# Six of eight GpSimd drains taken out behind the experts' scatters

## The chip, the cores and the metric

One core of one Trainium2 chip runs the whole program: TensorE (matrix products), VectorE, ScalarE, GpSimd and SyncE, and 16 DMA engines that they share. The metric is the device time of one execution in microseconds (us), as the median of several runs. In the profile the engines are called PE (TensorE), PEld (TensorE's weight loads), DVE (VectorE), ACT (ScalarE), POOL (GpSimd) and SP (SyncE); POOLq is GpSimd's sequencer, which takes the instructions in their written order and hands them to the engine.

## What is computed

A gated linear recurrence over 768 steps for 4 x 8 heads, whose output, 3,072 tokens of 384 numbers, goes through a layer of 8 experts. Each token goes to one expert alone.

```python
for t in range(S):                       # attention: a complex state per head
    S_re, S_im = ar * S_re - ai * S_im + k[t] v[t]^T, ar * S_im + ai * S_re
    y[t] = q[t] @ S_re
x = y.transpose(0, 2, 1, 3).reshape(3072, 384)
logits = x @ w_gate                      # 8 experts
expert_idx = argmax(logits); gate_w = softmax(logits)[expert_idx]
for e in range(8):
    xe = x[expert_idx == e]
    ye = relu(xe @ w1[e]) @ w2[e]        # 384 -> 1024 -> 384
    out[expert_idx == e] = gate_w * ye
```

## The kernel before

The program has two stages. The first (to about 220 us) is the recurrence in chunks of 128 steps; at its end every token has been sent by GpSimd's indirect DMAs into `xs_hbm`, one block of rows for each expert. The second stage, which the change touches, is the experts' layer. It runs over the experts as *ranks*, r = 0 to 7, the fullest expert first.

For a rank, SyncE loads the rows and the weights (`loads`), VectorE turns the rows (`turned`), and TensorE makes the first layer. `fast1` forms it from sums and differences of blocks, seven products in the place of eight; the sums of weights (tile `ws`) are GpSimd's, those of rows (also in `ws`) are VectorE's, and those of results (`um`) VectorE's too. The second layer is `fast2`, called for rank r - 1 while r is at its first layer. It multiplies 3 x 2 blocks with a scheme of fifteen products, written out step by step in `FIFTEEN` (line 114). A step "W7 12-0" is a difference of weight blocks 12 and 0 into W7 (block 13), made by GpSimd (line 998); "H..." is the same for hidden values, by VectorE; "P5 11+13" is a product of hidden block 11 with weight block 13 into bank 5, four matmuls on TensorE, each two instructions in the trace; "C..." are copies by ScalarE and "A..." sums by VectorE; "G..." scales a result into a `yo` tile. Blocks 0 to 5 are the rank's own weights (`w2b`) or hidden values (`ht`); the others are scratch, which lies in `w2b` or `wA` tiles and in `htA`. W7 and W5 are each written twice in a rank, so the second writing has to follow the product that reads the first: for W7 that is "P2 12+13", for W5 "P1 6=11". The second W5 and W7 are read by "P5 3+11" and "P5 11+13".

When 128 tokens of a rank are done, `sent` (line 782) has GpSimd send the rows of `yo` to their places in the output by an indirect DMA (line 673; the *scatter*). The tokens of ranks 0 to 4 beyond 384 are worked in two shared tiles (`shared`, called at r = 1 and r = 4); their scatters take the row numbers from `hs`, the others from `hg`. Some `yo` tiles lie in memory named `mask` and `turn`.

Behind each rank's work the loop adds a drain of GpSimd (line 1059): `nc.gpsimd.drain()`. It names the marks "scattered" and "drained" to the planner, so that it stays behind the scatters that were added before it and drains stay in order among themselves; the instruction itself carries no semaphore wait and no engine waits for it. It is an instruction of GpSimd's sequencer, and what is written behind it for GpSimd waits until it is over.

All operations of the stage are collected in a `Plan` (`M.add`), each with what it reads and writes, and then issued in the order that `EXPERTS` (line 86) lists by hand: 994 numbers to the base 36, the places of the operations in the collection. Each engine takes its own in that order. Where a helper makes the sums and products, the trace has the helper's line: 200 for every two-operand sum, 770 for `product`.

Of the kernel before, what the change touches and what calls it, by code (L numbers as in the profile page):

```python
# [18 lines left out]
N, DM, E, F = B * S, H * D, 8, 1024  # L19
# [64 lines left out]


EXPERTS = """
0 1 2 3 4 g 7 c 9 1e 38 h i l o p r u v 8 1q n m x t 1r z q 10 a w s 13 11 16 14 17 j 18 19 b 12 1n 5 1i 1u y 1a 15 1y 22 1o
1v 1f 1z 20 1s 1x 1p 6 26 21 24 23 25 1h 28 1b 1w 2a f 1g 27 2b 2c 2e 2i 2d 2g 2f 1j 2m k 2h 2n 2k 1c 2s 29 2v 2u 2j 2l 2t 2x
e 1t 2q 2y 31 2r ev 2z 4y 3h 3o 3i 3p 56 33 34 3s 3t 3k 3r 3l 4z 50 3m 2p 2o 2w 57 5a 30 32 54 3n 3j 35 58 59 3u 3v 3w 3y 3x
3z 41 3q 40 44 45 48 46 3a 72 47 4a 5b 39 3b 74 49 4b 42 4e 5e 43 4f 4d 4c 4k 4l 3c 3e 7c 5c 5d 7d 5g 4g 55 5f 5i 3d 5h 1k 5l  # L90
51 52 53 7e 4n 4h 5n 4j 5m 5o 75 5j 7f 4t 7h 5p 4x 5q 73 1d 36 5k 5u d 7b 5r 4m 6h 5s 1m 5w 5x 6a 5t 5y 60 5z 4s 61 6i 37 62
63 6q 64 65 66 7k 7i 5v 4q 6s 6r 76 6b 6c ay 6d 6j 4u 67 6t 4w 7j 6y b2 4v 6e 6f 6k 6l 6m 6n 6g 7m 4i 7q az 4p 7l 6u 6v 6w 7n
8s 7r 90 6x 6z 92 7o 7p 7s b7 8t 8u 7t 7u 7g 7y 7v 4o ik 91 94 93 7z b0 80 77 81 82 84 96 6o 95 97 4r 83 68 87 9a 98 99 7w 86
85 88 8b 8a 7x 8g 8j 89 8h 8k ab 8e 8f 9f 9c 9g 8y 8z 8v b9 8w 8x 9h 8m 8p 9b 9i ba 8n 8i 9d 9e ac b6 bf 9k 9o 8c 9j 9q 9l 9m
9r 9s 9u ak bd be a4 9t 9w 9n 9v 9y 7a 9x 9p 3g a5 9z a6 a7 al ad 8q 69 6p 8r bb a0 a1 bc b8 am cn co a8 cq cp cr an 79 a9 aa
ae ct b1 as af ag ao ap aq 8o ah aw bh bl bi bj bk bn f5 f3 b3 ax bg 8d a2 bm ar cu bp cv bq at cx bo br cw cs bt bu cy bx 8l
by bv f8 d1 cz d0 d3 d2 d4 bw c1 bz c0 c3 70 ai d5 d9 bs c4 f4 c2 cc d7 c9 cb ce c5 d6 d8 f6 ca ci c7 da db dc e6 cm dd cg e7
df de c6 dg dh dj c8 ex b5 dl dm 71 a3 dn do f7 dp di dq aj ch dk 78 dr au dt dv ds ew ef eg du dw fa dz e0 e2 ez ey cj e1 dx
f0 e3 e8 f2 e4 e9 ck eh ei ej en e5 ek el cd ea eb gj fb 1l em ec eq b4 eu fe ff cf fd fg gg gh it in fh av dy ed ee cl go eo
gq ep f9 il gp gs gr gu fi fj gt 3f fk gw fl gv fm fc gm gn fn fq fr fs er ft gi gk is gl gx h0 fu fy fv fw g2 fx fo no fp gy  # L100
gz h1 g0 g8 g1 fz g9 iv gb g6 gc h2 im g7 hz gd h3 h4 gf h5 h6 h8 hc h7 he iz g3 i0 np nq nr h9 ha hd hf es hg ga hh hi f1 hb
hj hk hl ip io ir hm g4 et ho hs j0 hn ht j1 hv ia i1 i8 hp ge hu i9 ib ns hw ig hx i2 hy k9 i3 i4 i5 j4 ix ic g5 hq j5 j8 iw
iy j6 id ie if mb iu ih ke j7 ja j9 jb j2 jc jd jg kf k6 k7 jh j3 kg je ji jj kc kd jk jl jm ki kh kk kj kl jo i6 jp jn jt km
jq js jf jr ko kn kp kq jw jz jv jx k8 k3 kt ku mc jy ks k1 kr ka kb lp kv li kw ky kx nt l2 kz md l4 lq l0 l3 ma mj l5 ly mh
m0 l6 l7 l8 l1 l9 la nu mi mk lb lz lc ld lj lk me ll k2 lr k5 m1 nv mf m6 k4 ml le lf hr i7 ju lm ln ls lt lu lv mg mm mn mo
lo m2 m3 mp m4 mq mu ms mr mv m5 k0 mt nw nx m7 ny nz o0 mw o1 my n2 mz n0 ps n3 mx o4 n1 lg n4 n7 pt o2 n5 pu o3 o5 pv ii iq
n6 n8 o6 na ij nc o8 ng p7 ni n9 o7 nh pw ne lh nk oa nf nl ob nj oc od p0 nn oe o9 og ok lw p8 nm of nb om oh oo nd oi on lx
m8 m9 q0 q1 pg oq op os oj or ou q2 q3 q4 q5 ot p1 ol ow ov ox ph p3 p4 p5 p9 p2 pi pj po pa pb pc px q8 pd qa pk p6 pl q9 pm
py pz pn pp qb qc pe qd qh q6 rc oy oz qj qx qe ql qf qk qn q7 qm qp qg qo qi r4 qr qq qy qs r0 r5 rd qt qu qz qv r1 r2 r3 re
rj pf pq r6 r7 rf r8 r9 ra pr qw rb rg rh ri rk rl  # L110
"""


# [73 lines left out]
def gateloop_then_moe(ctx, tc, gates, qk, gates_u, qk_u, v_u, v, wg, w1, w2, out):  # L187
    nc = tc.nc
# [13 lines left out]
    def const(shape, nm, val=None, dt=FP32):  # L202
        t = consts.tile(shape, dt, name=nm)
        if val is not None:
            nc.gpsimd.memset(t, val)
        return t
# [52 lines left out]
    lg = const([128, NT, E], "lg")  # L259


    with ExitStack() as att:
        ap = att.enter_context(tc.tile_pool(name="ap", bufs=1))

        def buf(nm, n, shape, dt=FP32):
            return [ap.tile(shape, dt, name=f"{nm}{i}") for i in range(n)]
        bAB, bZ = buf("AB", NB, [128, 2 * G * TU]), buf("Z", NZ, [128, G * 2 * TU])
        bC, cz = buf("C", NB, [128, G * TU]), buf("cz", NC, [128, G * 2 * TU])
        cm = buf("cm", 2, [112, 2 * 2 * TU])
        nc.vector.memset(cm[0][32:64], 0.0)  # L270
        vb = buf("v", NV, [128, 3, DM + D * len(SWAPPED)])
        am = buf("am", 4, [128, 4, 128])
        kt = buf("kt", 2, [128, 2, 384])
# [422 lines left out]
        with tc.manual_schedule():  # L696
            for u in range(NU):
                front(u)
                b, t0, t1 = UNITS[u]
# [7 lines left out]
                if u == NU - 3:  # L707
                    fa = early()
# [10 lines left out]
            for i in P.order(ORDER):  # L719
                o = P.ops[i]  # L720
# [11 lines left out]
    with ExitStack() as ms:  # L732
        mp = ms.enter_context(tc.tile_pool(name="mp", bufs=1, reuse_waits="tile"))
# [10 lines left out]
        ht = buf("ht", 2, [128, FT, 384])  # L744
        hl = buf("hl", 2, [128, FT, 128])
# [3 lines left out]
        hg = buf("hg", 3, [128, 3, 2])  # L749
        hs = buf("hs", 2, [128, 2])  # L750
# [15 lines left out]
        def pe(dur, fn, r, w):  # L766
            on_pe.append(M.add("PE", dur, fn, r, w, after=tuple(on_pe[-1:])))
# [182 lines left out]
        def tile2(r, j, k, k0=0):  # L950
            s = r % 2
            w, kw = w2_of(r)
            for h2 in range(2):
                def f(h2=h2):
                    for f_ in range(4 * h2, 4 * h2 + 4):
                        nc.tensor.matmul(bank[k][:, 0:DM], lhsT=ht[s][:, f_, j * 128 - k0:j * 128 - k0 + 128], rhs=w[:, f_ * DM:f_ * DM + DM],
                                         start=(f_ == 0), stop=(f_ == FT - 1))
                pe(2.6, f, (kw,) + tuple(("ht", s, f_, x) for f_ in range(4 * h2, 4 * h2 + 4) for x in range(2 if j else 1)), (("K", k),))
            finish(k, hg[r % 3][:, j, :], (("hg", r % 3),))
# [76 lines left out]
        def first_layer(r):  # L1036
            turned(r)
            if r == 0:
                late()
            (fast1 if r in FAST1 else layer1)(r)  # L1040

        with tc.manual_schedule():
            M.add("SP", 0.0, lambda: None, (), ("perm",))
            loads(0)
            for r in range(E + 1):
                if r + 1 < E:
                    loads(r + 1)
                if r < E:
                    first_layer(r)
                if r == 0:  # L1050
                    tile2(0, 2, 4, 256)
                if r == 1:
                    shared(0, 7)
                if r > 1:
                    fast2(r - 1)
                if r == 4:
                    shared(1, 5)
                if r < E:
                    M.add("POOL", 1.0, lambda: nc.gpsimd.drain(), ("scattered",), ("drained",))
                if r == 3:  # L1060
                    pe(0.2, lambda: nc.tensor.matmul(bank[5][0:1, 500:501], lhsT=okm, rhs=one, start=True, stop=True), ("okm",), (("K", 5),))
                    M.add("DVE", 0.2, lambda: nc.vector.tensor_scalar(out=again, in0=bank[5][0:1, 500:501], scalar1=127.5, scalar2=None, op0=ALU.is_lt), (("K", 5),), ("again",))
                if r == 4:
                    pe(0.5, lambda: flag.append(nc.values_load(again[0:1, 0:1], min_val=0, max_val=1, skip_runtime_bounds_check_because="0 or 1")), ("again",), ())
            for i in M.order(EXPERTS):
                M.ops[i]["fn"]()


    with tc.If(flag[0] > 0, preferred_fallthrough_block=False), ExitStack() as fs:  # L1069
        fp = fs.enter_context(tc.tile_pool(name="fp", bufs=1))  # L1070
# [5 lines left out]
        with tc.For_i(0, S, TB) as i0:  # L1076
            a = fp.tile([128, 2, B, G, TB], FP32, name="fa")
# [9 lines left out]
            af = a.rearrange("p u b g t -> p u (b g t)")  # L1087
# [12 lines left out]
            for t in range(TB):  # L1100
# [6 lines left out]
                z = {}  # L1107
# [5 lines left out]
                kv = fp.tile(shape, FP32, name="kv")  # L1113
# [14 lines left out]
        with tc.For_i(0, NT, 1) as ti:  # L1128
# [11 lines left out]
            l = fp.tile([128, E], FP32, name="l")  # L1140
            nc.vector.tensor_copy(l, bank[1][:, 0:E])
            m = fp.tile([128, 1], FP32, name="m")
            nc.vector.tensor_reduce(m, l, axis=AX, op=ALU.max)
            nc.vector.tensor_scalar(out=l, in0=l, scalar1=m, scalar2=None, op0=ALU.subtract)
            ex = fp.tile([128, E], FP32, name="fex")
# [5 lines left out]
            m2 = fp.tile([128, 1], FP32, name="fm2")  # L1151
# [4 lines left out]
            for e in range(E):  # L1156
# [4 lines left out]
                hh = fp.tile([128, FT, 128], FP32, name="hh")  # L1161
                for f_ in range(FT):
                    hb = bank[2 + f_ // 4][:, (f_ % 4) * 128:(f_ % 4) * 128 + 128]
                    for d in range(DT):
                        c = d * F + f_ * 128
# [57 lines left out]
```

## Time and profile before

| what | us |
|---|---|
| runs | 464.96, 465.85, 469.82 |
| median | 465.85 |
| profiled execution | 467.38 |
| its span, first to last instruction | 465.7 |
| mean granted TensorE clock | 0.994 of full speed |

The page's part 1 gives the busy time of each engine. TensorE is the busiest; GpSimd is busy for less than half of the span. Times in the rows are us from the span's start, durations of groups in ns where that is said. A row of a timeline is one instruction or several of a kind in succession: start, duration, engine, line, operation, written tile <- read tiles, shape, count, and in brackets the idle time of the engine ahead of it with what the profile takes for the releaser. A drain is work of the sequencer, not of the engine, so it is no busy time and stands in no timeline of the engine; it is found by its line.

### The profile page before, as it was taken

To read this page: it belongs to the slowest core of one execution; us is meant where nothing else is said; L and a number is where in the kernel's file an instruction comes from. 1 tells how busy PE (TensorE), PEld (TensorE's weight loads), DVE (VectorE), ACT (ScalarE), POOL (GpSimd) and SP (SyncE) were. 2 spreads that over 40 slices of the span, in tenths; PEclk is the share of its full clock that TensorE was granted. 3 is DMA by queue.
4 is the path that set the end of the run, shared out by engine and by line. 5 is a ranking of instruction groups with operands and counts; after the bars stand their busy time and mean duration, and the time that the engine had idled before them with its cause. 6 is when DMAs were issued, how large, how long until landed. Compare 5 with 4: busy or idle time off the path is not lost. (4 is left out here: it accounts for less than half of the span.)

```text
span 465.7 us, 12727 instructions
## 1 busy us (share of the span) xinstructions
PE 408.0 (88%) x5186; PEld 370.1 (79%) x5186; DVE 342.4 (74%) x623; ACT 290.7 (62%) x541; POOL 213.3 (46%) x256
## 2 busy tenths in 40 slices
PE   0142999989979998999999999899999999999994
PEld 0022788778869787898689799899997999999994
DVE  6999999999998999752443765475765655786762
ACT  5999999999998988743011333464636336346432
POOL 8100021027201545422044923666975949569664
PEclk9999999999999999999999999899999999999999
DMA  8355692866486662772793097804467152000102
GB/s 273 136 188 151 170 363 75 262 167 212 89 297 145 214 166 104 203 238 106 213 323 105 2 265 220 320 1 170 150 185 247 37 190 100 1 1 36 67 18 82
DMA packets 31554, 73.27 MB, mean 157 GB/s; under 512 B 19955, under 2 KB 21900, under 8 KB 28160
## 3 DMA queue, kind: packets, MB, share of 16 engines
q1 hardware_dynamic: 28160, 62.49, 44.2%
q0 software_dynamic: 3184, 9.86, 5.6%
q8 instruction: 43, 0.70, 0.6%
q14 instruction: 23, 0.19, 0.1%
q10 hardware_dynamic: 144, 0.03, 0.0%
HBM read 55.65 MB, written 12.29 MB: 146 GB/s over the span
## 5 line engine op out<-in xcount | busy, mean ns | idle before, releaser
L200 POOL TENSOR_TENSOR Z<-Z,C 128x1152 f32<-128x1152 f32 (+2 forms) x7 | 16.0, 2289 | 118.3 <-DVE Z L200 64.1
L200 DVE TENSOR_TENSOR um<-bank,um 128x432 f32<-128x432 f32 (+6 forms) x84 | 46.3, 566 | 31.5 <-PE bank L770 30.4
L770 PE MATMUL bank<-xrt,w1b 128*128 128x216 f32 (+6 forms) x336 | 68.6, 334 | 0.0
L770 PEld LDWEIGHTS bank<-xrt,w1b 128*128 128x128 f32 x336 | 58.2, 191 | 1.5 <-issue 0.6
L556 POOL DMA_INDIRECT xs_hbm<-xg,slot x24 | 32.4, 1352 | 37.3 <-issue 14.4
L300 ACT ACTIVATE AB<-AB 128x1152 f32<-128x1152 f32 (+5 forms) x46 | 45.5, 998 | 3.9 <-DVE first L613 1.8
L1009 ACT COPY bank<-ht 128x512 f32<-128x512 f32 x48 | 28.0, 589 | 22.5 <-DVE htA L200 14.4
L200 POOL TENSOR_TENSOR wA<-wA,w2b 128x512 f32<-128x512 f32 x22 | 28.2, 1289 | 25.6 <-PE bank L770 23.4
L422 PE MATMUL bank<-order,cz 128*128 128x128 f32 x60 | 11.1, 296 | 28.7 <-DVE cz L200 22.0
L200 DVE TENSOR_TENSOR am<-bank,mask 128x512 f32<-128x512 f32 x48 | 31.5, 679 | 3.6 <-PE bank L443 3.6
L200 DVE TENSOR_TENSOR Z<-Z,AB 128x1152 f32<-128x1152 f32 (+4 forms) x20 | 31.7, 1589 | 0.8 <-ACT AB L300 0.3
L770 PE MATMUL bank<-w2b,ht 128*128 128x128 f32 x240 | 31.2, 280 | 0.0
L435 PE MATMUL bank<-Z 48*64 48x128 f32 (+1 forms) x576 | 29.8, 254 | 1.2 <-DVE Z L200 1.2
L422 PEld LDWEIGHTS bank<-order,cz 128*128 128x128 f32 x60 | 7.0, 147 | 29.9 <-issue 22.3
L770 PE MATMUL bank<-ws 128*128 128x216 f32 (+6 forms) x168 | 30.7, 332 | 0.1
L723 ACT ACT_TABLE_LOAD x23 | 29.5, 1283 | 1.7 <-PEq L1208 1.3
L473 PE MATMUL bank<-am,v 128*48 128x128 f32 x384 | 26.1, 280 | 5.0 <-DVE am L200 5.0
L770 PEld LDWEIGHTS bank<-w2b,ht 128*128 128x128 f32 x240 | 29.7, 197 | 0.0
L435 PE MATMUL bank<-cz 48*64 48x64 f32 (+1 forms) x576 | 29.3, 261 | 0.4 <-DVE am L200 0.4
L770 PEld LDWEIGHTS bank<-ws 128*128 128x128 f32 x168 | 28.5, 190 | 0.4 <-POOL ws L200 0.4
L921 ACT ACTIVATE ht<-um 128x368 f32<-128x368 f32 (+9 forms) x42 | 20.9, 512 | 9.0 <-DVE um L200 9.0
L473 PEld LDWEIGHTS bank<-am,v 128*48 128x48 f32 x384 | 21.5, 126 | 5.8 <-DVE am L200 5.2
(250 smaller groups left out, 1158.9 us busy)
## 6 DMA issues: line engine op xcount, KB each, us to landing
w1b<-in_w_dram SPq DMA_DIRECT2D x7, 1536.0 KB, 7.5
w2b<-in_w_dram SPq DMA_DIRECT2D x7, 1536.0 KB, 10.3
AB<-in_gates_u_dram SPq DMA_DIRECT2D x6, 1152.0 KB, 5.9
Z<-in_qk_u_dram SPq DMA_DIRECT2D x6, 1152.0 KB, 7.8
v<-in_v_u_dram SPq DMA_DIRECT2D x8, 792.0 KB, 6.3
wA<-in_w_dram SPq DMA_DIRECT2D x4, 768.0 KB, 5.7
xs_hbm<-htA SPq DMA_DIRECT2D x2, 1045.0 KB, 9.1
xr<-xs_hbm SPq DMA_DIRECT2D x12, 156.0 KB, 4.8
```

The costliest lines, as they stand in the source:

```text
L200: return (eng or nc.vector).tensor_tensor(out=o, in0=a, in1=b, op=op)
L300: lambda: nc.scalar.activation(o, i, func=f, scale=scale, bias=bias, **kw), r, w, tag)
L422: nc.tensor.transpose(KT[part][:, g * 128:g * 128 + 128], wide[part][:, g, 1], order)
L435: nc.tensor.matmul(SC[h % 2][y:y + 64, g * 128 + x:g * 128 + 128], lhsT=wide[part][side(h), g, 1, x:x + 64], rhs=wide[part][side(h), g, 0, ...
L473: nc.tensor.matmul(YT[side(h), (h // 2) * 128:(h // 2) * 128 + 128], lhsT=values(h), rhs=am[2 * par + h % 2][:, h // 2, :], start=(c == 0 ...
L556: i = nc.gpsimd.indirect_dma_start(out=xs_hbm[:, :], out_offset=bass.IndirectOffsetOnAxis(ap=R[slot][:, c:c + 1], axis=0), in_=xg[:, (g0 + ...
L723: nc.scalar.preload_act_table_set("natural_log_exp_and_others" if P.cur == "LE" else "trig_and_small")
L770: nc.tensor.matmul(o, lhsT=l, rhs=x, start=start, stop=True, skip_group_check=True)
L921: M.add("ACT", 0.00094 * 2 * (hi - lo) + 0.16, lambda o=o, i=i: nc.scalar.activation(o, i, func=ACT.Relu), keys, ko)
L1009: M.add("ACT", 0.5, lambda o=blocks(bank[n], 1)[0], i=HO[int(a)]: nc.scalar.copy(o, i), HK[int(a)], (("K", n),))
```

## The change

The drain is added for r = 6 and r = 7 alone, the last two ranks. The six others leave the collection of operations, so the numbers of all later ones fall by one to six, and the list `EXPERTS` is written anew: it is the old list without the numbers 49, 115, 253, 391, 533 and 667 (in base 10), and the rest renumbered; the order of the remaining 988 operations is the same. No operation is added or moved.

```diff
 EXPERTS = """
-0 1 2 3 4 g 7 c 9 1e 38 h i l o p r u v 8 1q n m x t 1r z q 10 a w s 13 11 16 14 17 j 18 19 b 12 1n 5 1i 1u y 1a 15 1y 22 1o
+0 1 2 3 4 g 7 c 9 1d 36 h i l o p r u v 8 1p n m x t 1q z q 10 a w s 13 11 16 14 17 j 18 19 b 12 1m 5 1h 1t y 1a 15 1x 21 1n
...
 """
...
                 if r == 4:
                     shared(1, 5)
-                if r < E:
+                if r in (6, 7):
                     M.add("POOL", 1.0, lambda: nc.gpsimd.drain(), ("scattered",), ("drained",))
```

## Rows read from the trace of the kernel before

**Rows 1.** The page's part 1: busy time, share of the span, instructions.
```profile
PE 408.0 (88%) x5186; PEld 370.1 (79%) x5186; DVE 342.4 (74%) x623; ACT 290.7 (62%) x541; POOL 213.3 (46%) x256
```

**Rows 2.** Waits of PEld, 228 us to the end: us, times, longest us.
```profile
PEld bank L1030 <- issue: 5.6, 28, 0.3
PEld bank L770 <- POOL wA L200: 2.7, 2, 2.1
PEld bank L770 <- DVE htA L200: 0.6, 1, 0.6
PEld bank L770 <- POOL ws L200: 0.4, 1, 0.4
```

**Rows 3.** Table by stages: us; PE, PEld, DVE, ACT, POOL busy; PEclk, DMA, GB/s.
```profile
282.00:296.00 14.00, 12.06 (x108) 11.87 (x106) 7.92 (x19) 6.61 (x21) 4.94 (x5) 1.00 0.77 276
```

**Rows 4.** TensorE's timeline from 286 us: start, us, line, tiles, count [idle before].
```profile
286.66 1.06 PE L770 MATMUL bank<-wA 128*128 128x128 f32 x8
...
292.02 1.95 PE L770 MATMUL bank<-w2b,htA 128*128 128x128 f32 x16
295.92 1.67 PE L770 MATMUL bank<-wA 128*128 128x128 f32 x8 [1.94 <-POOL wA L200]
...
299.09 1.91 PE L770 MATMUL bank<-xrt,w1b 128*128 128x204 f32 x8
```

**Rows 5.** GpSimd's timeline from 286 us.
```profile
286.67 0.96 POOL L673 DMA_INDIRECT out_dram<-yo,hs  x1 [3.24 <-DVE mask L200]
287.63 1.30 POOL L200 TENSOR_TENSOR w2b<-w2b,w2b 128x512 f32<-128x512 f32 x1
294.60 1.26 POOL L200 TENSOR_TENSOR wA<-wA,w2b 128x512 f32<-128x512 f32 x1 [5.66 <-PE bank L770]
```

**Rows 6.** Line 1059, drains starting near 286 and 374 us (durations in ns).
```profile
L1059 POOLq DRAIN  x1: 8020/8020/8020, 286.5 to 286.5; - x1
...
L1059 POOLq DRAIN  x1: 9685/9685/9685, 374.7 to 374.7; - x1
```

**Rows 7.** DMA issues: the two scatters of shared tiles, us to landing.
```profile
out_dram<-yo,hs POOLq DMA_INDIRECT x1, 7.7
...
out_dram<-mask,hs POOLq DMA_INDIRECT x1, 7.5
```

**Rows 8.** Table by stages around 298 us; the granted clock is the third from last.
```profile
296.00:298.00 2.00, 2.00 (x11) 2.00 (x12) 0.09 (x1) 0.00 (x0) 1.92 (x2) 0.60 1.01 430
298.00:300.00 2.00, 2.00 (x11) 1.99 (x10) 0.00 (x0) 0.00 (x0) 1.92 (x3) 0.55 0.95 337
300.00:302.00 2.00, 2.00 (x13) 2.00 (x12) 0.73 (x3) 1.33 (x5) 2.00 (x2) 1.00 0.18 32
```

**Rows 9.** GpSimd's timeline: ranks 2 and 4, behind their drains.
```profile
341.82 0.99 POOL L673 DMA_INDIRECT out_dram<-yo,hg  x1 [1.27 <-issue]
...
376.68 0.92 POOL L673 DMA_INDIRECT out_dram<-mask,hs  x1 [0.16 <-DVE wA L200]
384.51 2.50 POOL L200 TENSOR_TENSOR wA<-wA,w2b 128x512 f32<-128x512 f32 x2 [6.92 <-PE bank L770]
```

**Rows 10.** TensorE's timeline from 377 us.
```profile
377.29 1.06 PE L770 MATMUL bank<-wA,htA 128*128 128x128 f32 x8
...
385.83 1.16 PE L770 MATMUL bank<-wA,ht 128*128 128x128 f32 x8 [0.34 <-POOL wA L200]
```

**Rows 11.** VectorE's timeline from 289 us.
```profile
289.15 0.64 DVE L200 TENSOR_TENSOR ws<-xrt 128x204 f32<-128x204 f32 x2
...
292.03 0.36 DVE L200 TENSOR_TENSOR ws<-xrt,ws 128x204 f32<-128x204 f32 x1
...
294.95 1.14 DVE L200 TENSOR_TENSOR ws<-xrt,ws 128x204 f32<-128x204 f32 x1
301.24 0.29 DVE L200 TENSOR_TENSOR mask<-bank,part 128x128 f32<-128x128 f32 x1 [5.15 <-ACT part L1012]
```

**Rows 12.** VectorE's groups by line and form: busy us, mean ns of one.
```profile
L200 DVE TENSOR_TENSOR htA<-htA,wA 128x512 f32<-128x512 f32 x1 | 3.1, 3105 | 0.0
```

More of the change, by code (lines that the diff above doesn't have):

```diff
@@ L86 @@
 EXPERTS = """
-0 1 2 3 4 g 7 c 9 1e 38 h i l o p r u v 8 1q n m x t 1r z q 10 a w s 13 11 16 14 17 j 18 19 b 12 1n 5 1i 1u y 1a 15 1y 22 1o
-1v 1f 1z 20 1s 1x 1p 6 26 21 24 23 25 1h 28 1b 1w 2a f 1g 27 2b 2c 2e 2i 2d 2g 2f 1j 2m k 2h 2n 2k 1c 2s 29 2v 2u 2j 2l 2t 2x
-e 1t 2q 2y 31 2r ev 2z 4y 3h 3o 3i 3p 56 33 34 3s 3t 3k 3r 3l 4z 50 3m 2p 2o 2w 57 5a 30 32 54 3n 3j 35 58 59 3u 3v 3w 3y 3x
-3z 41 3q 40 44 45 48 46 3a 72 47 4a 5b 39 3b 74 49 4b 42 4e 5e 43 4f 4d 4c 4k 4l 3c 3e 7c 5c 5d 7d 5g 4g 55 5f 5i 3d 5h 1k 5l
@@ L91 @@
[L91 to L110, printed above, removed]
+0 1 2 3 4 g 7 c 9 1d 36 h i l o p r u v 8 1p n m x t 1q z q 10 a w s 13 11 16 14 17 j 18 19 b 12 1m 5 1h 1t y 1a 15 1x 21 1n
@@ new lines @@
+1u 1e 1y 1z 1r 1w 1o 6 25 20 23 22 24 1g 27 1b 1v 29 f 1f 26 2a 2b 2d 2h 2c 2f 2e 1i 2l k 2g 2m 2j 1c 2r 28 2u 2t 2i 2k 2s 2w
+e 1s 2p 2x 30 2q eq 2y 4w 3f 3m 3g 3n 54 32 33 3q 3r 3i 3p 3j 4x 4y 3k 2o 2n 2v 55 58 2z 31 52 3l 3h 34 56 57 3s 3t 3u 3w 3v
+3x 3z 3o 3y 42 43 46 44 38 6z 45 48 59 37 39 71 47 49 40 4c 5c 41 4d 4b 4a 4i 4j 3a 3c 79 5a 5b 7a 5e 4e 53 5d 5g 3b 5f 1j 5j
+4z 50 51 7b 4l 4f 5l 4h 5k 5m 72 5h 7c 4r 7e 5n 4v 5o 70 35 5i 5s d 78 5p 4k 6f 5q 1l 5u 5v 68 5r 5w 5y 5x 4q 5z 6g 60 61 6o
@@ new lines @@
+62 63 64 7h 7f 5t 4o 6q 6p 73 69 6a au 6b 6h 4s 65 6r 4u 7g 6w ay 4t 6c 6d 6i 6j 6k 6l 6e 7j 4g 7n av 4n 7i 6s 6t 6u 7k 8p 7o
+8x 6v 6x 8z 7l 7m 7p b3 8q 8r 7q 7r 7d 7v 7s 4m ie 8y 91 90 7w aw 7x 74 7y 7z 81 93 6m 92 94 4p 80 66 84 97 95 96 7t 83 82 85
+88 87 7u 8d 8g 86 8e 8h a8 8b 8c 9c 99 9d 8v 8w 8s b5 8t 8u 9e 8j 8m 98 9f b6 8k 8f 9a 9b a9 b2 bb 9h 9l 89 9g 9n 9i 9j 9o 9p
+9r ah b9 ba a1 9q 9t 9k 9s 9v 77 9u 9m 3e a2 9w a3 a4 ai aa 8n 67 6n 8o b7 9x 9y b8 b4 aj cj ck a5 cm cl cn ak 76 a6 a7 ab cp
@@ new lines @@
+ax ap ac ad al am an 8l ae as bd bh be bf bg bj f0 ey az at bc 8a 9z bi ao cq bl cr bm aq ct bk bn cs co bp bq cu bt 8i bu br
+f3 cx cv cw cz cy d0 bs bx bv bw bz 6y af d1 d5 bo c0 ez by c8 d3 c5 c7 ca c1 d2 d4 f1 c6 ce c3 d6 d7 d8 e2 ci d9 cc e3 db da
+c2 dc dd df c4 es b1 dh di a0 dj dk f2 dl de dm ag cd dg 75 dn ar dp dr do er eb ec dq ds f5 dv dw dy eu et cf dx dt ev dz e4
+ex e0 e5 cg ed ee ef ej e1 eg eh c9 e6 e7 ge f6 1k ei e8 em b0 ep f9 fa cb f8 fb gb gc in ih fc du e9 ea ch gj ek gl el f4 if
@@ new lines @@
+gk gn gm gp fd fe go 3d ff gr fg gq fh f7 gh gi fi fl fm fn en fo gd gf im gg gs gv fp ft fq fr fx fs fj ni fk gt gu gw fv g3
+fw fu g4 ip g6 g1 g7 gx ig g2 hu g8 gy gz ga h0 h1 h3 h7 h2 h9 it fy hv nj nk nl h4 h5 h8 ha eo hb g5 hc hd ew h6 he hf hg ij
+ii il hh fz hj hn iu hi ho iv hq i5 hw i3 hk g9 hp i4 i6 nm hr ib hs hx ht k3 hy hz i0 iy ir i7 g0 hl iz j2 iq is j0 i8 i9 ia
+m5 io ic k8 j1 j4 j3 j5 iw j6 j7 ja k9 k0 k1 jb ix ka j8 jc jd k6 k7 je jf jg kc kb ke kd kf ji i1 jj jh jn kg jk jm j9 jl ki
@@ new lines @@
+kh kj kk jq jt jp jr k2 jx kn ko m6 js km jv kl k4 k5 lj kp lc kq ks kr nn kw kt m7 ky lk ku kx m4 md kz ls mb lu l0 l1 l2 kv
+l3 l4 no mc me l5 lt l6 l7 ld le m8 lf jw ll jz lv np m9 m0 jy mf l8 l9 hm i2 jo lg lh lm ln lo lp ma mg mh mi li lw lx mj ly
+mk mo mm ml mp lz ju mn nq nr m1 ns nt nu mq nv ms mw mt mu pm mx mr ny mv la my n1 pn nw mz po nx nz pp id ik n0 n2 o0 n4 n6
+o2 na p1 nc n3 o1 nb pq n8 lb ne o4 n9 nf o5 nd o6 o7 ou nh o8 o3 oa oe lq p2 ng o9 n5 og ob oi n7 oc oh lr m2 m3 pu pv pa ok
@@ L111 @@
+oj om od ol oo pw px py pz on ov of oq op or pb ox oy oz p3 ow pc pd pi p4 p5 p6 pr q2 p7 q4 pe p0 pf q3 pg ps pt ph pj q5 q6
+p8 q7 qb q0 r6 os ot qd qr q8 qf q9 qe qh q1 qg qj qa qi qc qy ql qk qs qm qu qz r7 qn qo qt qp qv qw qx r8 rd p9 pk r0 r1 r9
+r2 r3 r4 pl qq r5 ra rb rc re rf
 """
```

## The prediction

> **What bounds the kernel now.** I read the page's busy table first. TensorE is busy 88% of the span [rows 1], but that share is an average, and each of the other engines idles in the expert stage, so the question is where TensorE itself stands still. I then put all waits of TensorE's weight loads (PEld) from 228 us to the end into one answer [rows 2]. The largest line, 5.6 us in 28 pieces of at most 0.3 us, is the short issue time between the small matmuls of L1030 and waits for nobody. Two lines are waits for GpSimd: 2.7 us in two pieces, of which the longer is 2.1 us, and 0.4 us once. The rest are single waits for issue, VectorE and ScalarE, the longest of them 0.6 us. No wait for a DMA or for SyncE is among them. So from 228 us on TensorE sets the pace, and whatever this change can give must come out of the GpSimd lines of this table or out of TensorE's clock. That is the ceiling of the forecast: about 3.1 us of waits, and what they do to the clock.
>
> Next I looked for the stage that holds the 2.1 us. The table by stages has TensorE busy 12.06 of the 14 us from 282 to 296 us [rows 3]; 1.94 us are missing, and the TensorE timeline puts them in one place: the products in the row at 292.02 are over at 293.97 (292.02 + 1.95), and the next one starts at 295.92 and has waited 1.94 us for a GpSimd write of wA [rows 4]. The GpSimd timeline shows that write: the add at 294.60, 1.26 or 1.27 us long, with 5.66 us of idle time ahead of it [rows 5].
>
> **Why GpSimd idles there.** The profile puts the 5.66 us down to a TensorE product, and the reader should not follow it. In the list of steps this add is "W7 12-0" of rank 1. It overwrites a block that "P2 12+13" has to read first; that product has both operands in wA, and it is the row at 286.66, over at 287.72 [rows 4]. So the add could have started at 288.93, when GpSimd had finished the add at 287.63 (287.63 + 1.30) [rows 5]. What stands between is the drain of rank 1: it runs from 286.5 for 8.02 us, to 294.5 [rows 6], and 0.1 us later the add starts. The drain in turn ends with the landing of the scatter ahead of it: issued at 286.67 [rows 5], landed 7.7 us later, at 294.4 [rows 7]. The instruction on the engine took 0.96 us of that. A drain therefore does not wait only for GpSimd's adds; it holds the queue until the rows that the scatter sent have arrived, and these scatters share the DMA engines with the next rank's weights.
>
> **The change, part by part.** Nothing is added, no wait is new, and no DMA moves past another in any queue. Six drains go; the order of all else stays. Of six I find two that touch TensorE.
>
> Rank 1's drain. Without it W7 starts at 288.93 and is over by 290.2, while TensorE asks for it after the products that end at 293.97: 3.8 us of cover. The stall goes whole. Its size by start times: 48 matmuls lie between the rows at 286.66 and 292.02, so one takes 5.36 / 48 = 0.1117 us; the 16 of the row at 292.02 would hand over at 293.81, and the next started at 295.92: 2.1 us [rows 4].
>
> The clock behind it. In the two stretches that follow the stall the granted clock is 0.60 and 0.55 of full speed, and 1.00 from 300 us on [rows 8]: TensorE sits at the lower of its two levels (1.2 against 2.4 GHz) for most of 4 us. The engine had been busy without a break until the stall, and nothing else happened to it. Lost: 2 x 0.40 + 2 x 0.45 = 1.7 us. Bounds: 0, if the clock falls anyway, and 1.7. I take 1.7, since the only break in TensorE's work near it is the one that goes.
>
> Rank 4's drain. It runs from 374.7 for 9.69 us [rows 6] behind a scatter that took 7.5 us to land [rows 7]. The add behind it is "W5 10+3"; it needs "P1 6=11", the row at 377.29, over at 378.35 [rows 10]; GpSimd is free at 377.60 (376.68 + 0.92) and starts it at 384.51 [rows 9], 6.1 us after it could. TensorE wants it for "P5 3+11": 72 matmuls after 377.29 would bring it there at 385.33, and it starts at 385.83 [rows 10]. That is 0.5 us. GpSimd then works through its adds without a pause, so the same lateness carries to the wait for ws of 0.4 us [rows 2], of which some 0.1 us is a normal step: 0.3 us.
>
> The other four. Rank 0's drain holds the scatter at 286.67 back: GpSimd idles 3.24 us ahead of it [rows 5]. No wait of TensorE goes back to a scatter [rows 2]. Ranks 2, 3 and 5 leave GpSimd idle about as long as the 1.27 us ahead of the scatter at 341.82 [rows 9], and no wait of TensorE for GpSimd lies in their stretches: both pieces of wA and the one of ws are spent above. So all four cost nothing now. What hides them is that GpSimd's adds run ahead of TensorE; were that lead gone, they would cost at most their idle time, 1 to 3 us each. Taken: 0.
>
> The sum: 2.1 + 1.7 + 0.5 + 0.3 = 4.6 us. The profiled execution takes 467.38 us (span 465.7 and 1.7 around it), so it would take 462.8. The median of the runs is 1.5 us lower, 465.85; the same 4.6 us off gives 461.25, call it **461.3**. That the gain lives to the end rests on rows 2: behind 300 us TensorE waits for nothing that does not move with it, and the two drains that stay belong to ranks 6 and 7, whose scatters no weights run beside.
>
> **Two rules of the Trainium skill that speak against it.** The row says that the scatter of 128 rows of 1,536 bytes landed after 7.7 us [rows 7]. The Trainium skill, "DMA: Bandwidth & Descriptors", section "Anatomy of one DMA — SWDGE (gpsimd) path", has about 2.0 us plus the bytes at 436 GB/s for one such DMA, which makes an estimate of 2.5 us here: the drain would have been over at 289.1, 0.2 us after the add before it, and the change would be worth nothing. The trace disagrees by 5 us, and the row decides.
>
> The other concerns the engine beside. VectorE's difference ws<-xrt,ws took 0.36 us at 292.03, while GpSimd stood still, and 1.14 us at 294.95, beside GpSimd's adds [rows 11]; a sum of the same kind (all three blocks in SBUF) once took 3.1 us [rows 12]. So VectorE's work is held up by GpSimd's, and today's idle time of GpSimd is a free lane for VectorE. The Trainium skill, "SBUF — State Buffer", section "SBUF: two separate sides", says why: such a VectorE instruction and a GpSimd one take turns on a shared pair of ports, whole instructions at a time. The rows agree.
>
> **The rivals.** First, *the stall goes and the slow clock stays* (or the usual execution has no slow clock there): gain 2.9 us, 462.95. Against it: no other break of TensorE's near. Second, *nothing comes of it*: GpSimd itself can't go on while the scatter's rows are under way, or the late landing is peculiar to the profiled execution; the stall stays or was never there, and 0 to 0.8 us come off, 465.4. Against it: the add at 287.63 ran right behind the scatter, 6 us before its rows arrived [rows 5, 7], and both scatters of this kind landed late, by 7.7 and 7.5 us. Third, on the other side, *VectorE pays*: GpSimd's adds move from 294.6 on to 288.9 on, over the two differences into ws from 289.15 on and the one at 292.03, which VectorE had to itself. At 0.8 us each (1.14 - 0.36) they are 2.4 us late, which the idle time between VectorE's instructions there and the 5.15 us that it stands still after 296.1 [rows 11] take up. It turns bad from the point where each takes the 3.1 us of the longest row: 3 x 2.7 = 8.1 us late. TensorE's next rank, whose first product starts at 299.09 today [rows 4], would come some 3.5 us sooner and then wait some 6, with a slow clock of 1.7 us behind it: 4.6 gained, 7.7 lost, 469. For it: the rows just named [rows 11, 12]. Against it: the 3.1 us stand once among all of VectorE's sums, and VectorE's instructions after 292 us follow TensorE's products, not GpSimd's.
>
> **How the numbers follow.** The forecast 0.70 (its own range 460.3 to 462.3: the clock's share and the pace of a run without the profiler); slow clock stays 0.12; nothing 0.10; VectorE pays 0.08. The predicted time is that of the first. The range 460.2 to 465.6 holds the first two and half of the third; left out are VectorE's case, the upper half of the third and a thin lower edge: under 2 in 10. One per cent, about what a measurement of this kernel can tell from no change, is 4.66 us here: the forecast stands almost on that line, so its 0.70 is cut in two, 0.36 below 461.19 and 0.34 above. Faster by over 1% 0.36; within 1% 0.34 + 0.12 + 0.10 and the milder half of VectorE's case, 0.60; slower by over 1% 0.04.
>
> **What would show it.** In the profile of the changed kernel two drains of L1059, both after 420 us. The add W7 of rank 1 within 0.2 us of the one before it, some 6 us ahead of the scatter's landing; no idle time of TensorE over 0.3 us from 282 to 300 us, and a granted clock of 1.00 throughout; no wait for wA or ws in PEld's table. The span near 461. Wrong would be: a wait of TensorE for VectorE's ws or um that is new and over 1 us; the slow clock in another place; or the landings of the two late scatters holding GpSimd without any drain.

## The result, and the profile after

The changed kernel takes 461.88 us (median of 6 runs, 460.83 to 462.42), the kernel before beside it 466.30 (6 runs, 464.87 to 471.10). The ratio is 0.9895 with a 95% interval of 0.9858 to 0.9932: 4.4 us or 1.05% faster, where 461.3 was forecast. A second comparison, with 11 more runs of the changed kernel and 33 of the one before, has 0.9941 (0.9910 to 0.9972), some 2.7 us. Both intervals hold gains from 3.2 to 4.2 us; why a gain of this kind is not one number is told with the clock below.

The profiled execution of the changed kernel takes 461.99 us, its span is 460.3. First the waits of TensorE's weight loads (PEld) from 228 us to the end: engine, tile and line, what was waited for, us in total, times, longest.

```profile
PEld bank L1030 <- issue: 5.6, 28, 0.3
PEld bank L770 <- issue: 0.6, 1, 0.6
PEld bank L770 <- DVE ws L200: 0.6, 1, 0.6
PEld bank L770 <- DVE um L200: 0.5, 1, 0.5
```

Both lines of [rows 2] that name GpSimd are gone, and nothing has taken their place: the 0.6 us for VectorE is the wait that [rows 2] has under htA (at 266.6 us before, at 266.0 now), and the 0.5 us behind 400 us stood in the kernel before too. The stage that held the longest wait [rows 3], and the two stretches behind it [rows 8], as a table by stages (us; PE, PEld, DVE, ACT, POOL busy; granted clock, DMA share, GB/s):

```profile
282.00:296.00 14.00, 14.00 (x124) 14.00 (x123) 9.78 (x19) 6.68 (x22) 11.65 (x10) 1.00 0.78 285
292.00:296.00 4.00, 4.00 (x35) 4.00 (x34) 2.75 (x8) 2.06 (x7) 3.92 (x4) 1.00 0.99 421
296.00:300.00 4.00, 4.00 (x26) 4.00 (x25) 3.09 (x7) 3.66 (x10) 1.60 (x2) 1.00 0.92 349
```

TensorE is busy without a break from 282 to 300 us, at a granted clock of 1.00. GpSimd's timeline of the same place, to be laid beside [rows 5]:

```profile
282.98 0.96 POOL L673 DMA_INDIRECT out_dram<-yo,hs  x1 [0.16 <-DVE wA L200]
283.93 1.31 POOL L200 TENSOR_TENSOR w2b<-w2b,w2b 128x512 f32<-128x512 f32 x1
287.19 1.27 POOL L200 TENSOR_TENSOR wA<-wA,w2b 128x512 f32<-128x512 f32 x1 [1.96 <-PE bank L770]
```

W7 is the sum at 287.19. It starts when "P2 12+13" has read its block, 6.0 us before TensorE asks for it (the product at 293.19), and so 4.7 us before it is needed complete. The scatter at 282.98 lands after 4.0 us, where it took 7.7 [rows 7]:

```profile
out_dram<-yo,hs POOLq DMA_INDIRECT x1, 4.0
```

Of L1059 two drains are left, both late:

```profile
L1059 POOLq DRAIN  x2: 5141/5844/6547, 430.1 to 447.1; - x2
```

For rank 4, "P1 6=11" starts at 372.83 and "P5 3+11" at 380.87, 8.04 us apart; before it was 385.83 - 377.29 = 8.54 [rows 10]. The half microsecond is there.

To compare executions on different chips, whose first 240 us differ by up to 11 us, I use one more measure, the *rest*: from the first product of rank 1's first layer (the first row of TensorE's timeline that reads w1b) to the end of the span. Before it is 465.7 - 245.16 = 220.5 us, after 460.3 - 244.55 = 215.8, a difference of 4.8 where the sum of the prediction is 4.6. The rests of all kernels below, each of one execution:

| kernel | rest | TensorE's wait for W7 (or what stands for it) | half clock in the rest, ahead of the last product |
|---|---|---|---|
| before | 220.5 | 2.1 | 3.4 us |
| after, after_again | 215.8, 215.8 | 0, 0 | none |
| r1_out | 216.5 | 0 | none |
| r0_out | 216.5 | 0 | none |
| r4_out | 217.9 | 2.1 | none |
| r235_out | 218.7 | 2.9 | none |
| twice | 221.2 | 2.3 | 3.4 us |
| loads_later | 220.6 | 2.7 | 3.4 us |
| loads_wait | 216.5 | 0 | none |
| warm | 217.0 | 0 | none |
| busy | 219.8 | 2.3 | 3.4 us |
| busy10 | 216.8 | 0.8 | none |
| all_out | 221.1 | 0 (2.3 for another) | 3.4 us |

### The profile page after: what moved, and what is told of

It reads as the page before. It is cut to its first block, busy times and chain, and to the rows that moved or that the text cites. A ratio compares the mean times of both kernels' runs of the same rounds, so it can differ in the third digit from the quotient of the medians.

```text
span 460.3 us, 12721 instructions
## 1 busy us (share of the span) xinstructions
PE 405.4 (88%) x5186; PEld 368.0 (80%) x5186; DVE 345.9 (75%) x623; ACT 290.5 (63%) x541; POOL 213.8 (46%) x256
```

## The experiments

In all of them EXPERTS stays the list of the kernel before unless said; a drain that is taken out is an operation that issues nothing.

**Which drain? (r1_out, r0_out).** One drain out, seven stay.

```diff
-M.add("POOL", 1.0, lambda: nc.gpsimd.drain(), ("scattered",), ("drained",))
+M.add("POOL", 1.0, (lambda: None) if r in (1,) else (lambda: nc.gpsimd.drain()), ("scattered",), ("drained",))
```

Rank 1 (r1_out):

> Rank 1's drain alone is taken out of the kernel before; seven stay. Theory A (the sum of the prediction: each drain is charged with the TensorE wait that it ends): the wait of 2.1 us for W7 and the 3.4 us at half clock go, so 3.8 us less than before, a median near 462.5; rank 4's waits of 0.5 and 0.3 us stay. Rival B (the drain of rank 0 is the cause as well, because it holds the scatter of rank 1 back into the weight loads): the same 3.8 us, since the drain that ends the wait is out. Rival C (the clock falls there without the stall): 2.1 us less.

Rank 0 (`r in (0,)`):

> Rank 0's drain alone is taken out; rank 1's stays. Theory A: no change, since no wait of TensorE goes back to rank 0's drain (the wait for W7 stays at some 2 us, the clock falls behind it), a median near 466.3. Rival B: without rank 0's drain the scatter of rank 1 is issued some 3 us sooner, ahead of the weight loads, lands after about 4 us as in the changed kernel (issued 282.98, 4.0 us) and not after 7.7; rank 1's drain then ends near 287.8, 0.2 us after GpSimd's add, W7 is not late, and this one drain is worth the whole 3.8 us: near 462.5.

Measured: r1_out 0.9949 (0.9922 to 0.9976), 2.4 us less; r0_out 0.9945 (0.9909 to 0.9981), 2.6 us less. The 3.8 us that were expected lie in the interval of r0_out (0.9 to 4.3) and just outside that of r1_out (1.1 to 3.7); the share of the clock in them is told below. Both rests are 216.5, the changed kernel's 215.8 and rank 4's two waits of 0.3 and 0.4 us; neither has the wait for W7. So rival B is right and the prediction's entry for rank 0 is wrong: rank 0's drain, at which no wait of TensorE ends, is worth as much by itself as rank 1's, and the two don't add. GpSimd's timeline of r0_out and its drain of rank 1 show why:

```profile
291.11 1.27 POOL L200 TENSOR_TENSOR ws<-w1b,ws 128x512 f32<-128x512 f32 x1 [2.35 <-PE bank L770]
292.54 0.96 POOL L673 DMA_INDIRECT out_dram<-yo,hs  x1 [0.15 <-DVE wA L200]
293.50 1.29 POOL L200 TENSOR_TENSOR w2b<-w2b,w2b 128x512 f32<-128x512 f32 x1
297.63 1.28 POOL L200 TENSOR_TENSOR wA<-wA,w2b 128x512 f32<-128x512 f32 x1 [2.84 <-PE bank L770]
```

```profile
L1059 POOLq DRAIN  x1: 4395/4395/4395, 293.1 to 293.1; - x1
```

The scatter follows the sum before it after 0.15 us, not 3.24 [rows 5]. Rank 1's drain still stands behind it, but takes 4.4 us and not 8.0 (the landing of this scatter has no record); W7 starts at 297.63, 0.95 us after the end of the product that it has to follow (295.62 + 1.06), and 3.8 us of cover take that.

**Why does it matter when the scatter is issued? (loads_later, loads_wait).** The suspect was the weight load w1b that SyncE issues at 286.10 in the kernel before, 0.6 us ahead of the scatter at 286.67 [rows 5]:

```profile
286.10 0.36 SPq L818 DMA_DIRECT2D w1b<-in_w_dram  x1
```

In both kernels all drains stay, and SyncE issues two small loads ahead of that load (numbers of operations in base 10); in loads_wait the hs load is issued twice there.

```diff
-... 259 ... 262 124 261 397 ...
+... 261 397 259 ... 262 124 ...
```

> The kernel before with all eight drains; only SyncE's order changes: two small loads (hs and one of xr) are issued ahead of the weight load w1b that stands near 286 us, not behind it, so that the weights start some 1.2 us later and the scatter of rank 1 is issued ahead of them. If weights on the DMA engines are what makes that scatter land late, it lands after about 3 us (not 7.7), the drain behind it ends near 290, W7 is in time and 2.1 to 3.8 us go. If the drain is long for another reason, the wait of 2 us for W7 stays and the time is that of the kernel before.

> All eight drains; as the run in which SyncE issues hs and xr ahead of the weight load, which put that load 0.5 us behind the scatter and left the landing late; now hs is loaded twice there, so that the weight load comes 1 to 3 us behind the scatter. In the other runs the scatters that landed in 2.9 and 4.0 us were issued 0.95 and 3.1 us ahead of the weight load. If weights on the DMA engines make it late, the scatter lands after 3 to 4 us, rank 1's drain takes about 4 and not 8 us, and W7 is in time. If not, the landing stays at 7 to 8 us and the wait of 2 us for W7 stays.

loads_later: 1.0004 (0.9979 to 1.0030). The load came 1.1 us later against the stage than before, but that put it only 0.5 us behind the scatter, which landed after 8.3 us all the same, and W7 was waited for by 2.7 us. The run missed the distance that it was made for. loads_wait: 0.9946 (0.9897 to 0.9994), 2.6 us less; here the load comes 2.9 us behind the scatter, rank 1's drain (the shorter of the two below, which are those of ranks 0 and 1) takes 3.05 us, and the wait is gone with all eight drains in place:

```profile
293.42 2.71 SPq L800 DMA_DIRECT2D hs<-xs_hbm  x2
296.35 0.33 SPq L791 DMA_DIRECT2D xr<-xs_hbm  x1
296.95 0.36 SPq L795 DMA_DIRECT2D w1b<-in_w_dram  x1
```

```profile
294.05 0.96 POOL L650 DMA_INDIRECT out_dram<-yo,hs  x1 [3.24 <-DVE mask L177]
295.01 1.30 POOL L177 TENSOR_TENSOR w2b<-w2b,w2b 128x512 f32<-128x512 f32 x1
297.01 1.30 POOL L177 TENSOR_TENSOR wA<-wA,w2b 128x512 f32<-128x512 f32 x1 [0.69 <-PE bank L747]
```

```profile
L1036 POOLq DRAIN  x2: 3054/3330/3607, 289.5 to 293.9; - x2
```

Ordered by the distance, from the timelines of SyncE (issue of w1b) and GpSimd (scatter) and from the drain's line, the scatters of the two shared tiles:

| kernel, rank | scatter against the weight load | landing | drain behind it |
|---|---|---|---|
| before, 1 | 0.57 us behind | 7.7 | 8.0 |
| before, 4 | 0.02 ahead | 7.5 | 9.7 |
| loads_later, 4 | 0.04 ahead | 6.9 | 9.1 |
| loads_later, 1 | 0.52 ahead | 8.3 | 8.6 |
| r235_out, 4 | 0.94 ahead | no record | 5.1 |
| after_again, 4 | 0.94 ahead | 2.5 | none |
| after, 4 | 0.95 ahead | 2.9 | none |
| warm, 1 | 1.67 ahead | no record | 3.8 |
| loads_wait, 1 | 2.90 ahead | no record | 3.1 |
| after, 1 | 3.09 ahead | 4.0 | none |
| r0_out, 1 | 3.11 ahead | no record | 4.4 |

What decides is how far ahead of the weight load the scatter is issued: 0.5 us was too little, 0.9 enough. (The second layer's weights, w2b, are issued 0.6 to 1.5 us behind w1b, so the two loads aren't told apart.) A late scatter begins late: in the kernel before, the 16 DMA engines are busy with SyncE's loads (q1) for 96% of the 4.6 us behind the scatter's issue, and none of its packets is among them; its 64 packets (q0, 0.09 MB) all come in the 3.2 us after that. In loads_wait all 64 are through 2.9 us behind the issue. DMA queues of the kernel before, from 286.7 to 291.3 and from 291.3 to 294.5 us (packets, MB, share of the 16 engines):

```profile
q1 hardware_dynamic: 498, 1.49, 96.1%
```

```profile
q0 software_dynamic: 64, 0.09, 7.6%
```

The Trainium skill, "DMA: Bandwidth & Descriptors", section "Anatomy of one DMA — SWDGE (gpsimd) path", gives an estimate of 2.2 us for a scatter of 0.09 MB: with weights behind it the trace comes near (2.5 to 4.0), with weights beside or ahead of it it is three times that and more (6.9 to 8.3).

**Does a drain cost anything by itself? (twice).** Two drains in each of the eight places.

```diff
-lambda: nc.gpsimd.drain()
+lambda: (nc.gpsimd.drain(), nc.gpsimd.drain())
```

> The kernel before with two drains in a row at each of the eight places. The first of a pair waits for whatever it waits for; the second finds nothing outstanding and shows what a drain costs by itself. Sum of the prediction: a drain costs by what it waits for, so the second takes under 0.3 us, and the time is that of the kernel before. Rival: a drain has a price of its own of 1.6 us or more (the shortest of the eight), then GpSimd is later by that at each place, and the wait for W7 grows by it.

0.9981 (0.9956 to 1.0006). Line 1059, the pair of rank 0 (ns, shortest, median, longest):

```profile
L1059 POOLq DRAIN  x2: 41/1826/3612, 282.1 to 285.7; - x2
```

The second of the pair takes 41 ns; it is the shortest of all 16 too. What a drain costs is what it waits for.

**Why is rank 0's drain long? (warm).** It takes 3.6 us with no scatter under way, and ends 2.3 us after GpSimd's last sum (285.74 and 283.44 in the kernel before). This kernel has all eight drains and a ninth, in GpSimd's idle time before.

```diff
 for i in M.order(EXPERTS):
     M.ops[i]["fn"]()
+    if i == 183:
+        nc.gpsimd.drain()
```

> The kernel before with all eight drains and one drain more, put behind GpSimd's fourth sum in a row that ends near 268 us, ahead of 8.9 us in which GpSimd idles anyway. Open was why rank 0's drain takes 3.6 us with no scatter under way. The traces so far suggest that the first drain that a program runs in this stage takes longer: rank 6's took 5.26 us where others ran before it and 6.55 us where it was the first (changed kernel), and rank 1's ended 1.9 us behind its scatter's last packet where it was the first and 0.4 us behind where it wasn't. If that is so, rank 0's drain falls from 3.6 to about 1.5 us here, the scatter of rank 1 goes out some 2 us sooner, ahead of the weight loads, lands in 4 us or so, rank 1's drain ends in time, and a kernel with one drain MORE is 2.9 to 3.8 us faster than before, since the extra drain lies in idle time. Rival: rank 0's drain waits for something that is late at that place; then it stays 3.6 us long, the wait for W7 stays 2.1 us or so and the time is that of the kernel before.

0.9905 (0.9870 to 0.9940): 4.5 us faster with a drain more (2.8 to 6.2; by the rests 3.5). The ninth (line 1068) takes the 3.6 us, where nobody waits; rank 0's (line 1059) falls to 1.36:

```profile
L1068 POOLq DRAIN  x1: 3625/3625/3625, 274.5 to 274.5; - x1
```

```profile
L1059 POOLq DRAIN  x1: 1362/1362/1362, 289.4 to 289.4; - x1
```

```profile
289.44 1.27 POOL L200 TENSOR_TENSOR ws<-w1b,ws 128x512 f32<-128x512 f32 x1 [3.33 <-PE bank L770]
291.71 0.96 POOL L673 DMA_INDIRECT out_dram<-yo,hs  x1 [1.00 <-DVE xrt L834]
292.67 1.30 POOL L200 TENSOR_TENSOR w2b<-w2b,w2b 128x512 f32<-128x512 f32 x1
295.43 1.28 POOL L200 TENSOR_TENSOR wA<-wA,w2b 128x512 f32<-128x512 f32 x1 [1.46 <-PE bank L770]
```

The scatter goes out 1.0 us after the sum, 1.7 us ahead of the weight load (293.38), rank 1's drain ends at 295.3 and W7 starts 0.1 us later, in time. So the first drain of the stage takes some 2 us longer than a later one in its place. It shows at rank 0 (3.6 against 1.36 us), and at rank 6: as the first it takes 6.55 us in the changed kernel and ends 2.2 us after the landing of the last scatter written ahead of it; in r235_out, with the two scatters issued at the same distance from its start but other drains before it, it takes 4.67. What the chip does in these 2 us is not shown by any run and stays open.

**Ranks 4 and 2, 3, 5 (r4_out, r235_out).** `r in (4,)` and `r in (2, 3, 5)`.

> Rank 4's drain alone is taken out. Theory A: the waits of 0.5 us for P5 3+11 and 0.3 us for ws go, 0.8 us less, near 465.5; the drain of rank 1 with its 2.1 us wait and its half clock stays. Rival B has the same here.

> The drains of ranks 2, 3 and 5 are taken out; 0, 1, 4, 6, 7 stay. Theory A: no change, near 466.3. Rival D (a drain far ahead of rank 4 makes its scatter late, as in the changed kernel that scatter is issued 0.9 us sooner against the stage and lands after 2.9 us, not 7.5): the scatter of rank 4 lands early, its drain is short, and 0.8 us go, near 465.5.

r4_out: 1.0016 (0.9987 to 1.0044), an interval of -0.6 to +2.1 us; r235_out: 0.9978 (0.9948 to 1.0009), -2.5 to +0.4. Neither time tells 0.8 us from 0; the -0.8 us lies just outside the interval of r4_out, whose runs had a lower mean granted clock (median 0.989) than the kernel before beside them (0.995), in places that its one trace doesn't show. The traces decide better. PEld's waits for GpSimd in r235_out:

```profile
PEld bank L770 <- POOL wA L200: 2.9, 1, 2.9
```

Both of rank 4's waits are gone, with rank 4's drain still there: its scatter is issued 0.94 us ahead of the weight load (383.42 and 384.36) and the drain takes 5.1 us, not 9.7. In r4_out the same two waits are gone, and its rest of 217.9 is the changed kernel's 215.8 and the 2.1 us wait. So rival D holds: the 0.8 us belong to either of two causes, as with rank 1.

**Late, but without a drain (busy, busy10).** As the changed kernel, but where rank 1's drain stood GpSimd works on a tile of its own.

```diff
+spare = mp.tile([128, 296], FP32, name="spare")
...
-M.add("POOL", 1.0, lambda: nc.gpsimd.drain(), ("scattered",), ("drained",))
+M.add("POOL", 1.0, (lambda: [tt(spare, spare, spare, ALU.add, nc.gpsimd) for z in range(12)]) if r == 1
+      else (lambda: nc.gpsimd.drain()) if r in (6, 7) else (lambda: None), ("scattered",), ("drained",))
```

> As the changed kernel (only the last two drains stay), but where rank 1's drain stood GpSimd makes 12 sums of 128 x 296 numbers in a tile that nothing else uses, some 9 us of work. No drain and no scatter holds GpSimd here, it is simply late. If what counts is only how late W7 comes, TensorE waits some 2 us for it again, and the time is 2 to 4 us above the changed kernel's. If the half clock belongs to such a stall, the trace shows the granted clock at one half behind it; if it comes only in some executions, it may show 1.00 throughout. Rival: a drain also does something to TensorE that sums don't, then the time stays that of the changed kernel.

> As the run with 12 sums of 0.75 us in the place of rank 1's drain, with 10: W7 comes 1.5 us sooner, and of the wait of 2.3 us about 0.8 us is left. The time lies 1.5 us below that run's if the clock does the same in both. If a short wait leaves the clock alone, the granted clock is 1.00 behind it and another 1.7 us come off.

busy: 1.0017 (0.9987 to 1.0047), that is 3.5 us above the changed kernel (0.9941 beside the same kernel before), all of its gain gone without one of the six drains. busy10: 0.9885 (0.9822 to 0.9948; four runs). The rests are 219.8 and 216.8; 215.8 + 2.3 + 1.7 makes 219.8, 215.8 + 0.8 makes 216.6. Clock of busy, and of r4_out, which has a like stall, in the table by stages:

```profile
293.00:295.00 2.00, 0.39 (x3) 0.39 (x4) 1.54 (x3) 0.96 (x3) 2.00 (x3) 1.00 0.97 412
295.00:297.00 2.00, 2.00 (x16) 2.00 (x16) 0.00 (x0) 0.00 (x0) 1.92 (x2) 0.77 1.04 442
297.00:299.00 2.00, 2.00 (x8) 1.98 (x8) 0.00 (x0) 0.45 (x2) 1.92 (x3) 0.50 0.81 262
299.00:301.00 2.00, 2.00 (x12) 2.00 (x11) 1.58 (x4) 1.60 (x7) 2.00 (x2) 0.88 0.06 14
```

```profile
300.00:302.00 2.00, 0.29 (x3) 0.10 (x1) 1.55 (x5) 1.09 (x3) 1.10 (x1) 1.00 0.97 412
302.00:304.00 2.00, 1.78 (x16) 1.78 (x16) 0.40 (x1) 0.00 (x0) 1.92 (x3) 1.00 1.05 449
304.00:306.00 2.00, 2.00 (x14) 2.00 (x13) 0.10 (x1) 0.94 (x4) 1.92 (x2) 1.00 0.90 346
306.00:308.00 2.00, 2.00 (x13) 2.00 (x13) 1.97 (x6) 1.69 (x5) 2.00 (x3) 1.00 0.29 45
```

In both TensorE is idle for most of the first row (1.6 and 1.7 us). In busy the granted clock is 0.77, 0.50 and 0.88 afterwards, at the lower of its two levels (1.2 against 2.4 GHz) for 3.4 us in all; in r4_out it stays at 1.00. Over all traces, a wait of 2.1 to 2.9 us was followed by the lower level in five (before, twice, loads_later, busy, all_out) and not in two (r4_out, r235_out); in the two with a wait of 0.7 or 0.8 us (warm at rank 4, busy10) and in the five without one it was not.

**The last two drains (all_out).** All eight are out.

> All eight drains are taken out, the last two too. Sum of the prediction: no weights run beside the scatters of ranks 6 and 7, and no wait of TensorE goes back to GpSimd behind 420 us, so the time is the changed kernel's, 2.9 to 4.6 us below the kernel before. Rival: the drains of ranks 6 and 7 (6.6 and 5.1 us) hold scatters back that end the program, then up to 5 us more come off.

0.9998 (0.9956 to 1.0041): no faster than before, and some 2.7 to 4.9 us slower than the six-drain change (0.9941 and 0.9895 of theirs). The rest is 221.1. Of TensorE, in its timeline near 449 us:

```profile
447.14 1.95 PE L770 MATMUL bank<-w2b,w2b 128*128 128x128 f32 x16
451.24 1.78 PE L770 MATMUL bank<-wA,w2b 128*128 128x128 f32 x8 [2.15 <-DVE w2b L200]
452.82 2.96 PE L770 MATMUL bank<-w2b,ht 128*128 128x128 f32 x16
```

It stands still for 2.15 us, waiting for a sum of VectorE's, and then runs at half clock. VectorE and GpSimd ahead of that:

```profile
443.25 5.20 DVE L200 TENSOR_TENSOR htA<-ht,htA 128x512 f32<-128x512 f32 x2
...
450.41 0.68 DVE L200 TENSOR_TENSOR w2b<-bank,ht 128x512 f32<-128x512 f32 x1
```

```profile
443.35 1.31 POOL L200 TENSOR_TENSOR wA<-wA,w2b 128x512 f32<-128x512 f32 x1
444.58 1.29 POOL L200 TENSOR_TENSOR wA<-wA 128x512 f32<-128x512 f32 x1
445.80 1.30 POOL L200 TENSOR_TENSOR wA<-wA,w2b 128x512 f32<-128x512 f32 x1
```

The two sums htA<-ht,htA at 443.25 take 5.20 us, while GpSimd works from 443.35 to 447.10. In the changed kernel the same two stand like this, with GpSimd idle until 436.78 behind rank 6's drain:

```profile
432.93 1.49 DVE L200 TENSOR_TENSOR htA<-ht,htA 128x512 f32<-128x512 f32 x2
...
436.67 0.68 DVE L200 TENSOR_TENSOR w2b<-bank,ht 128x512 f32<-128x512 f32 x1
```

That is the prediction's third rival, VectorE's sums held up by GpSimd's, at rank 6 and not at rank 1. The Trainium skill, "SBUF — State Buffer", section "SBUF: two separate sides", has such instructions of the two engines take turns on a shared pair of ports; the trace agrees (5.20 against 1.49 us). So rank 6's drain, at which no wait of TensorE ends, keeps GpSimd away from VectorE. (This kernel has no drain of rank 7 either, and no run takes out one of the two alone; but in the changed kernel rank 7's starts at 447.1 us, behind these sums.) The stall and the clock are 2.3 + 1.7 = 4.0 of the 5.3 us by which this rest lies above the changed kernel's. The other 1.3 lie behind the last product: there the program's closing drain (line 1219), which is now the first drain of the stage, takes 5.4 us and not 3.5.

**The changed kernel again (after_again).**

> The changed kernel again, beside the kernel before on the chip of the other runs. If the 1.7 us of half clock belong to every execution of the kernel before, the difference is 4.6 us (ratio 0.990); if the clock falls behind the stall only in some executions, it lies between 2.9 us (0.994) and 4.6. In the trace: no wait of TensorE for GpSimd from 228 us on.

0.9941 (0.9910 to 0.9972), 1.3 to 4.2 us. No wait for GpSimd, rest 215.8. The point lies at the lower bound of what was expected, the interval reaches over most of it.

## Why the prediction was right, and where it was not

*Where the time was.* Right. All of it came out of the two GpSimd lines of [rows 2] and the clock; no wait appeared elsewhere, and the rest fell by 4.8 us against a sum of 4.6.

*Rank 1's drain ends the stall, 2.1 us.* Right in size: r4_out's rest lies 2.1 us above the changed kernel's with nothing but this stall. It was not the only cause. The signs "within 0.2 us of the one before it" and "some 6 us ahead of the scatter's landing" failed: in the changed kernel W7 comes 1.96 us after the sum before it, held by its product, and 0.2 us after the landing (282.98 + 4.0), because scatter and sum moved 3.1 us ahead against the stage (282.98 - 244.55 = 38.4, before 286.67 - 245.16 = 41.5). I had left them where they were.

*The clock, 1.7 us.* Right for the profiled execution and as a mechanism (busy brings the stall and the lower level back, without a drain). Wrong as a constant: the lower level followed such a stall in five of seven traces. Taken so, an estimate of the gain of an average execution is 2.1 + 0.8 + 5/7 x 1.7 = 4.1 us, which lies in both measured intervals; 4.6 lies only in the first. For rank 1's stall alone it is 3.3 and not 3.8 us, which the intervals of r1_out and r0_out hold. Seven traces of seven kernels are few for such a share. The rival "the slow clock stays" was not an alternative to the forecast but its other share.

*Rank 4, 0.8 us.* Right in the traces (8.54 to 8.04 us between the two products, and no wait for ws), too small for the times of single-drain runs. As with rank 1, its drain is not the only cause (r235_out). (GpSimd starts "W5 10+3" 6.2 us after it could, by 384.51 - 378.35, and not 6.1; no term hangs on it.)

*"The other four cost nothing."* Wrong, and this is the step to learn from. I charged each drain with the TensorE wait that ends on it, and rank 0's had none. But it held a scatter back by 3.2 us into the weight loads, and that is what made rank 1's drain long. [rows 5] shows both, 3.24 us of idle time ahead of the scatter and 7.7 us to its landing in [rows 7]; I used the first as harmless and the second as given. Ranks 2, 3 and 5 stand in the same way behind rank 4's. The sum came out right only because all of them were taken out together: then each wait is counted once, whichever cause it is charged to.

*Drains wait for landings.* Right, with an addition: a drain that finds nothing to wait for takes 41 ns, and the first of the stage takes some 2 us longer than the same drain with another before it. The estimate of 2.5 us that was set against it counted 128 rows of 1,536 bytes, 197 KB; the trace has 0.09 MB for this scatter, which makes 2.2 and changes nothing in the argument.

*VectorE pays.* In the changed kernel VectorE did pay, and had the time. These are its differences into ws, to be laid beside [rows 11]:

```profile
288.54 2.74 DVE L200 TENSOR_TENSOR ws<-xrt 128x204 f32<-128x204 f32 x2
...
292.00 0.65 DVE L200 TENSOR_TENSOR ws<-xrt,ws 128x204 f32<-128x204 f32 x1
...
294.34 0.90 DVE L200 TENSOR_TENSOR ws<-xrt,ws 128x204 f32<-128x204 f32 x1
```

The first two take 2.74 us where they took 0.64, the next 0.65 and not 0.36, and TensorE never waits for them. The same mechanism costs 4.0 us, nearly the whole gain, once the last two drains go as well. That rank 6's drain has this use the prediction did not see; it held the two that stay only for harmless.

## What to carry to other kernels

A barrier is to be charged with the wait that ends on it and also with what it holds back: a DMA issued 3 us later can meet other transfers and make the next barrier long, and then removing either brings the whole, not its half. Before a barrier is taken out, look at which other engine ran faster while it stood. Where the first of several barriers is long for no wait that shows, one more, placed where its engine idles anyway, can take that time. And a stall's effect on the clock is a chance, not a constant: one trace with the dip is no ground to count it in full.

## What the runs showed that was not expected

A kernel with nine drains was 4.5 us (2.8 to 6.2) faster than with eight, and one with none was no faster than with eight. The first drain of the stage took 3.6 us with no scatter under way, in the same place but not the first 1.4, and a second one right behind another 0.04. Scatters issued 0.9 us or more ahead of a weight load landed after 2.5 to 4.0 us, those issued from 0.6 us behind it to 0.5 ahead after 6.9 to 8.3. Stalls of the same 2.1 us were followed by 3.4 us at the lower clock in one trace and by none in another.
